# A three-stage attention, gated MLP and expert kernel: three widths of an expert's first-layer group for five, and four buffers for raw weights for two

## The chip, the cores and the metric

The kernel runs on one core of a Trainium2 chip. The metric is the device time of one execution in microseconds (us). The comparison is with the kernel before the change, 794.81 us as the median of three runs.

## What is computed

Four sequences of 576 tokens go through an attention with 8 heads of 64 (with a bias from running sums of `s`), a gated MLP over a width of 512, and a layer of 8 experts, of which each token uses one. The expert layer, the one that the change touches, is cut from the reference here:

```python
logits = np.einsum('bsd,de->bse', x, w_gate)
...
for b in range(B):
    prev_e = -1
    for s in range(S):
        fresh_e = int(np.argmax(logits[b, s]))
        ...
        h = np.maximum(x[b, s] @ w1[e], 0.0)
        out[b, s] = p[e] * (h @ w2[e])
```

`w1[e]` is 512 x 1024 and `w2[e]` 1024 x 512. A second gate decides whether a token takes its own best expert or that of the token before it. How many of the 2304 tokens an expert gets is known only on the chip.

## The kernel before, in words

The program is one stream of instructions for each engine. A scheduler puts them in order when the program is built, from its own estimate of times, within what data, buffers and a few `behind(...)` lines allow; each engine then runs its stream in that order. Attention, the MLP and the routing take the first 500 us and some; the change doesn't touch them. Before the MLP has ended, expert 0's first 256 tokens are fetched and their first layer is run (`early_fetch`, `early_xT`, `early_L1`, lines 1387 to 1409). Its result, the early hT, is a tile `hTA` of 128 x 2 x 8 x 256 numbers in the pool `wpool`; `early_L2` reads it.

**Tokens.** For each expert up to three blocks of 128 tokens are gathered by an indirect DMA on POOL (`gather`, line 1275), turned with PE into `xT` (line 1281), and split there into a rounded high part and the rest, since every product is made of three: high x high, high x rest, rest x high.

**Weights.** `load_w(e, j)` (line 1244) brings one eighth of an expert's weights, 512 KB: `j` 0 to 3 are the first layer's, 4 to 7 the second's. SP issues the DMA into a raw buffer (`wraw`, two of them), ACT casts it into the high part of a `wp` tile (line 1256), and DVE subtracts to get the rest (line 1257). The raw buffer is free when DVE is done, the `wp` tile (ten in turn, four in one pool and six in the other) when PE has used it. `next_w` says in `experts` (line 1438) where each load stands: (e,6), (e,7), (e+1,0) and (e+1,1) after the groups `LW` of expert e's first layer, (e+1,2) and (e+1,3) after it, (e+1,4) and (e+1,5) after its second layer.

**First layer.** `L1` (line 1310) makes eight groups `f` of 128 hidden units, each of 12 matmuls into one PSUM buffer (`ps`, seven in turn). ACT takes the relu into `hT` (line 1340), DVE the rest (line 1341). For experts 1 to 7 the 12 matmuls stand in the program five times, for 256, 288, 320, 352 and 384 columns of tokens, and PE branches to one by the expert's class `wide[e]`, which `emit_wide` counts from the token numbers (`choose`, lines 1327 to 1337). The first matmul of a group always has 384 columns. In this run the widths of experts 1 to 7 are 384, 320, 256, 288, 288, 320 and 352.

**Second layer.** `L2` (line 1347) makes 128 tokens by 24 matmuls, scales them, and scatters them to the output with an indirect DMA on POOL. The third block has three forms by `tail[e]`: none, a narrow one of 16 matmuls on a copy in a tile `xTA`, or the full 24. In this run expert 3 has none, experts 2, 4, 5 and 6 the narrow one, 1 and 7 the full one. The transposes for the next expert stand between the two layers. Beside expert 3, a few small instructions make a list for tokens beyond three blocks (`emit_olist`).

Expert 0 is not in `wide`. SP's queue is in order: an issue that waits for its raw buffer holds those behind it.

Of the kernel before, what the change touches and what calls it, by code (L numbers as in the profile page):

```python
# [8 lines left out]
F32 = mybir.dt.float32  # L9
# [4 lines left out]
ALU = mybir.AluOpType  # L14
# [10 lines left out]
def f32v(ap):  # L25
    return ap.bitcast(F32)
# [7 lines left out]
def kernel(  # L34
# [19 lines left out]
    PE, ACT, DVE, POOL, SP = nc.tensor, nc.scalar, nc.vector, nc.gpsimd, nc.sync  # L54
# [10 lines left out]
    KD = DM // 128  # L65
# [11 lines left out]
    def dma(out, in_):  # L77
        return SP.dma_start(out=raw(out), in_=raw(in_))
# [3 lines left out]
    def behind(x, name):  # L82

        tc.add_manual_dep(
            x.ins, name, mybir.DependencyInfo(mybir.DependencyClass.NoSync, mybir.DependencyReason.DATA), reason="after"
        )
# [12 lines left out]
    def rs():  # L99
        return ps("rt", 1)  # L100
# [15 lines left out]
    def T(pool, shape, dt, tag, bufs=1):  # L116
        _n[0] += 1
        return pool.tile(shape, dt, tag=tag, name=f"{tag}_{_n[0]}", bufs=bufs)
# [1122 lines left out]

    WP = {}

    def load_w(e, j):

        r = T(wpool, [128, 1024], F32, "wraw", bufs=2)
        if j < KD:
            dma(r, w1[e, 128 * j:128 * j + 128, :])
        else:
            f0 = 256 * (j - KD)  # L1250
            x = dma(r.rearrange("p (a d) -> p a d", a=2), w2[e, f0:f0 + 256, :].rearrange("(a p) d -> p a d", p=128))
            if e == 0:
                behind(x, m_loads[LPN])
        near = (e * 2 * KD + j) % (WA + WB) < WA
        w = T(wpool if near else epool[0], [128, 2, 1024], F32R, "wp", bufs=WA if near else WB)
        c = ACT.copy(out=w[:, 0, :], in_=r)  # L1256
        a = DVE.tensor_tensor(out=w[:, 1, :], in0=r, in1=f32v(w[:, 0, :]), op=ALU.subtract)  # L1257
        if (0, KD) <= (e, j) < (1, KD):
            behind(a, dmarks[-1].ins.name)
        if (1, 0) < (e, j) < (1, 2 * KD):  # L1260
            behind(c, amarks[1 if j < KD else 3].ins.name)
        WP[e, j] = w

    CC = CAP * 128
# [24 lines left out]
            DVE.tensor_tensor(out=xt[:, 1, kt, 0:w], in0=pt[:, 0:w], in1=f32v(xt[:, 0, kt, 0:w]), op=ALU.subtract)  # L1289

    LW = (0, 2, 4, 6)
    WIDE = (256, 288, 320, 352, CC)
    wide, tail = {}, {}

    def emit_wide(pool):

        pt = rs()
        PE.matmul(pt[:, 0:E], lhsT=onesb, rhs=carry, start=True, stop=True)
        cls = T(pool, [128, 2, E], F32, "cls")
        cli = T(pool, [128, E], I32, "cli")  # L1300
        DVE.tensor_copy(out=cls[:, 0], in_=pt[:, 0:E])
        DVE.tensor_scalar(out=cls[:, 1], in0=cls[:, 0], scalar1=float(WIDE[0]), scalar2=None, op0=ALU.is_gt)
        for x in WIDE[1:-1]:
            DVE.scalar_tensor_tensor(out=cls[:, 1], in0=cls[:, 0], scalar=float(x), in1=cls[:, 1], op0=ALU.is_gt, op1=ALU.add)
        DVE.tensor_copy(out=cli, in_=cls[:, 1])
        for e in range(1, E):
            wide[e] = PE.value_load(cli[0:1, e:e + 1])
            tail[e] = nc.values_load(cli[0:1, e:e + 1], engines=[mybir.EngineType.PE, mybir.EngineType.Activation, mybir.EngineType.DVE])

    def L1(e, xt, ht, w_, after={}):  # L1310
        for f in range(NF):
            pt = ps()
            fs = slice(128 * f, 128 * f + 128)

            def products(c):
                pairs = []
                for kt in range(KD):
                    w = WP[e, kt]
                    pairs += [(w[:, 0, fs], 0, kt), (w[:, 0, fs], 1, kt), (w[:, 1, fs], 0, kt)]
                for n, (l, z, kt) in enumerate(pairs):  # L1320
                    a = w_ if n == 0 else c
                    m = PE.matmul(pt[:, 0:a], lhsT=l, rhs=xt[:, z, kt, 0:a], start=(n == 0), stop=(n == len(pairs) - 1))  # L1322
                    if n == 0 and f in after:
                        behind(m, after[f].ins.name)

            if e in wide:
                def choose(a, z):
                    if z - a == 1:
                        products(WIDE[a])
                        return  # L1330
                    m = (a + z) // 2
                    with tc.If(wide[e] < m) as x:
                        choose(a, m)
                    with x.Else():
                        choose(m, z)

                choose(0, len(WIDE))
            else:
                products(w_)
            ACT.activation(out=ht[:, 0, f, 0:w_], in_=pt[:, 0:w_], func=ACTF.Relu)  # L1340
            DVE.scalar_tensor_tensor(out=ht[:, 1, f, 0:w_], in0=pt[:, 0:w_], scalar=0.0, in1=f32v(ht[:, 0, f, 0:w_]), op0=ALU.max, op1=ALU.subtract)  # L1341
            yield 12 * w_ * 0.42
# [218 lines left out]
    for b in range(B - 1):  # L1561
        m = M_steps(b) if b else M0_steps()
# [12 lines left out]
    wpool = wctx.enter_context(tc.tile_pool(name="wpool", bufs=1, side="right"))  # L1575
# [21 lines left out]
    x = fetch(early["xg2"], ids[:, CAP - 1:CAP])  # L1597
# [36 lines left out]
```

## Time and profile before

| | us |
|---|---|
| median of 3 runs (794.74 to 808.97) | 794.81 |
| the profiled execution | 794.49 |
| its span, first to last instruction | 792.6 |
| PE busy in the span | 752.5 |
| DVE, ACT, POOL busy | 527.9, 434.0, 344.5 |
| experts 1 to 7, from 551.67 to about 784 | 232.3 |

The profile comes from one execution, so sums are made against 794.49 us. PE is the matmul engine, DVE the vector engine, ACT the scalar engine; POOL and SP issue DMAs. A matmul's end is modelled, and neighbouring matmuls overlap, so a row's us can reach a little into the next row. "Issue" as a releaser means that the profile shows nothing for which the engine waited. The granted clock is 1.00 at 2.4 GHz and 0.50 at 1.2 GHz. A row of the timeline that merges matmuls of several widths shows the width of the first.

### The profile page before, as it was taken

The page shows a single profiled execution, that of the slowest core. Times are in us where ns is not written, and L with a number is a line of the kernel's source. Part 1 is how long each engine was busy: PE and PEld are TensorE (multiplying, and loading weights), DVE is VectorE, ACT ScalarE, POOL GpSimd, SP SyncE. Part 2 cuts the span into 40 slices and gives each one's busy share as a digit, 9 for nine tenths or more (in the row PEclk, how much of TensorE's full clock was granted, in tenths as well). Part 3 has the DMA queues.
Part 4 walks back from the last instruction along what each step waited for, and adds up shares of the span by engine and source line. Part 5 has one row for each costly group of instructions (what it writes and reads, how often), then busy time and mean ns, then how long its engine had stood idle before and what let it go on. Part 6 is the DMA issues. An engine that isn't in the chain of part 4 may idle for free. (4 is left out here: it accounts for less than half of the span.)

```text
span 792.6 us, 14859 instructions
## 1 busy us (share of the span) xinstructions
PE 752.5 (95%) x4763; PEld 643.7 (81%) x4763; DVE 527.9 (67%) x1493; ACT 434.0 (55%) x1039; POOL 344.5 (43%) x616
## 2 busy tenths in 40 slices
PE   9988998999999999999999999999999789998895
PEld 5666786799889899898898879787988678888694
DVE  6888577885776889696986777675535456555440
ACT  6777676875447876266973354145434444453431
POOL 6688545775525687335784020070122222412211
PEclk9999999999999999999999999999999999999998
DMA  7888689666688485688441952164363553753521
GB/s 184 207 235 238 149 230 280 158 184 158 157 247 220 107 240 120 168 254 198 108 155 33 343 168 94 61 195 167 96 206 101 185 176 128 215 160 122 182 65 38
DMA packets 118066, 133.46 MB, mean 168 GB/s; under 512 B 69603, under 2 KB 83043, under 8 KB 117963
## 3 DMA queue, kind: packets, MB, share of 16 engines
q1 hardware_dynamic: 114123, 122.61, 56.1%
q0 software_dynamic: 3840, 9.48, 3.4%
q8 instruction: 64, 1.05, 0.5%
q14 instruction: 39, 0.32, 0.1%
HBM read 90.99 MB, written 22.95 MB: 144 GB/s over the span
## 5 line engine op out<-in xcount | busy, mean ns | idle before, releaser
L1257 DVE TENSOR_TENSOR wp<-wraw,wp 128x1024 fp32r<-128x1024 f32 x64 | 80.3, 1260 | 72.9 <-ACT wp L1256 65.0
L1322 PE MATMUL ps<-xT,wp 128*128 128x320 f32 (+4 forms) x672 | 106.8, 317 | 13.8 <-issue 8.6
L1322 PEld LDWEIGHTS ps<-xT,wp 128*128 128x128 f32 x672 | 102.6, 193 | 17.6 <-issue 11.1
L1256 ACT CAST wp<-wraw 128x1024 fp32r<-128x1024 f32 x64 | 67.0, 1051 | 78.8 <-DMA wraw<-in_moe_w_dram 76.4
L447 ACT ACTIVATE E<-E,negm 128x128 f32<-128x128 f32 (+4 forms) x136 | 79.2, 584 | 33.7 <-DVE negm L440 21.6
L451 POOL TENSOR_SCALAR E<-E,lsum 128x128 f32<-128x128 f32 (+4 forms) x136 | 81.2, 600 | 36.2 <-DVE lsum L449 29.4
L887 PE MATMUL ps<-wp,hT 128*128 128x512 f32 x408 | 95.7, 394 | 1.2 <-DVE hT L1430 0.6
L887 PEld LDWEIGHTS ps<-wp,hT 128*128 128x128 f32 x408 | 76.0, 188 | 17.9 <-DVE hT L1430 1.1
L572 PE MATMUL ps<-et,vv 128*128 128x320 f32 (+9 forms) x462 | 79.5, 310 | 2.3 <-DVE et L539 1.2
L440 DVE CUSTOM_DVE_ANT_0 E<-ps,zmask 128x128 f32<-128x128 f32 (+4 forms) x136 | 63.5, 471 | 23.4 <-PE ps L887 18.0
L572 PEld LDWEIGHTS ps<-et,vv 128*128 128x128 f32 (+1 forms) x462 | 63.1, 173 | 15.4 <-DVE et L539 2.1
L532 PE MATMUL ps<-ident,E 128*128 128x128 f32 (+1 forms) x452 | 67.9, 262 | 4.8 <-POOL E L451 3.2
L1380 POOL DMA_INDIRECT out_dram<-y,ids x24 | 27.9, 1162 | 95.8 <-ACT y L1357 65.8
L448 POOL TENSOR_SCALAR lsum<-lsum 128x1 f32<-128x1 f32 (+1 forms) x128 | 29.6, 231 | 91.8 <-ACT E L447 79.8
L887 PE MATMUL ps<-wsg,vg 128*128 128x288 f32 x448 | 67.5, 300 | 0.6 <-DVE g L896 0.3
L541 ACT CAST et<-ps 128x384 fp32r<-128x384 f32 (+3 forms) x120 | 50.5, 428 | 29.3 <-PE ps L532 27.9
L887 PEld LDWEIGHTS ps<-wsg,vg 128*128 128x128 f32 x448 | 61.0, 188 | 1.4 <-DVE g L896 0.6
L532 PEld LDWEIGHTS ps<-ident,E 128*128 128x128 f32 (+1 forms) x452 | 47.5, 141 | 15.0 <-POOL E L451 4.9
L542 DVE TENSOR_TENSOR et<-ps,et 128x384 fp32r<-128x384 f32 (+3 forms) x120 | 56.8, 482 | 3.9 <-ACT et L541 3.5
L887 PE MATMUL ps<-w,vg 128*128 128x512 f32 (+1 forms) x216 | 56.8, 403 | 0.0
L887 PE MATMUL ps<-xh,w 128*128 128x288 f32 x240 | 54.9, 306 | 0.8 <-DVE wsg L870 0.7
L1341 DVE SCALAR_TENSOR_TENSOR hT<-ps,hT 128x384 fp32r<-128x384 f32 x56 | 30.0, 552 | 34.6 <-ACT hT L1340 34.6
(329 smaller groups left out, 1615.4 us busy)
## 6 DMA issues: line engine op xcount, KB each, us to landing
wraw<-in_moe_w_dram SPq DMA_DIRECT2D x64, 512.0 KB
qk<-qk SPq DMA_DIRECT2D x24, 432.0 KB
w<-wv_d SPq DMA_DIRECT2D x16, 512.0 KB
w<-wo_d SPq DMA_DIRECT2D x16, 512.0 KB
qk<-qk SPq DMA_DIRECT2D x24, 288.0 KB
w<-wu_d SPq DMA_DIRECT2D x11, 512.0 KB
nq<-in_q_dram SPq DMA_DIRECT2D x30, 144.0 KB
nk<-in_k_dram SPq DMA_DIRECT2D x30, 144.0 KB
```

The costliest lines, as they stand in the source:

```text
L440: hred[g] = DVE.tensor_tensor_reduce(out=e[:, a:z], in0=pt[:, 0:z - a], in1=zmask[:, m0:m0 + z - a], scale=-1.0, scalar=BIG if hi == 0 els ...
L447: ACT.activation(out=x, in_=x, func=ACTF.Exp, scale=-1.0, bias=nm, accum_out=l[:, z:z + 1])
L451: POOL.tensor_scalar(out=x, in0=x, scalar1=l[:, z:z + 1], scalar2=1.0, op0=ALU.mult, op1=ALU.mult)
L532: PE.transpose(pt[:, j * M:(j + 1) * M], e[h, 128 * j:128 * (j + 1)], ident[h, h])
L541: ACT.copy(out=dst[0], in_=src)
L542: DVE.tensor_tensor(out=dst[1], in0=src, in1=f32v(dst[0]), op=ALU.subtract)
L572: PE.matmul(x, lhsT=l, rhs=rhs if g >= F4 else f32v(rhs), start=(j == 0 and n_ == 0), stop=(j == js[-1] and n_ == len(ms) - 1),)
L887: ms = [PE.matmul(pt, lhsT=l, rhs=r, start=(first_ and x == 0), stop=(last_ and x == n - 1)) for x, (l, r) in enumerate(pairs)]
L1256: c = ACT.copy(out=w[:, 0, :], in_=r)
L1257: a = DVE.tensor_tensor(out=w[:, 1, :], in0=r, in1=f32v(w[:, 0, :]), op=ALU.subtract)
L1322: m = PE.matmul(pt[:, 0:a], lhsT=l, rhs=xt[:, z, kt, 0:a], start=(n == 0), stop=(n == len(pairs) - 1))
L1341: DVE.scalar_tensor_tensor(out=ht[:, 1, f, 0:w_], in0=pt[:, 0:w_], scalar=0.0, in1=f32v(ht[:, 0, f, 0:w_]), op0=ALU.max, op1=ALU.subtract)
```

## The change

Three widths are left: 288, 320 and 384. The class is counted against 256, 288 and 320, so an expert with up to 256 tokens now uses 288 columns and one with 321 to 352 uses 384. PE tests class < 2, then class < 3. From the weight (1,6) on, the loads whose number 8e + j is 2 or 3 modulo 4 go into a tile with room for two raw weights, with the tag `hTA`, that is in the place of the early hT; the others go on using the two `wraw` buffers.

```diff
--- before.py
+++ after.py
@@ -1241,9 +1241,18 @@
 
     WP = {}
 
+    RW = 4 * KD - 2
+    raws = []
+
     def load_w(e, j):
 
-        r = T(wpool, [128, 1024], F32, "wraw", bufs=2)
+        n = 2 * KD * e + j
+        if n >= RW and n % 4 > 1:
+            if not raws:
+                raws.append(T(wpool, [128, 2, 1024], F32, "hTA"))
+            r = raws[0][:, n % 2, :]
+        else:
+            r = T(wpool, [128, 1024], F32, "wraw", bufs=2)
         if j < KD:
             dma(r, w1[e, 128 * j:128 * j + 128, :])
         else:
@@ -1289,7 +1298,8 @@
             DVE.tensor_tensor(out=xt[:, 1, kt, 0:w], in0=pt[:, 0:w], in1=f32v(xt[:, 0, kt, 0:w]), op=ALU.subtract)
 
     LW = (0, 2, 4, 6)
-    WIDE = (256, 288, 320, 352, CC)
+    STEP = (256, 288, 320)
+    WIDE = ((2, 288), (3, 320), (4, CC))
     wide, tail = {}, {}
 
     def emit_wide(pool):
@@ -1299,8 +1309,8 @@
         cls = T(pool, [128, 2, E], F32, "cls")
         cli = T(pool, [128, E], I32, "cli")
         DVE.tensor_copy(out=cls[:, 0], in_=pt[:, 0:E])
-        DVE.tensor_scalar(out=cls[:, 1], in0=cls[:, 0], scalar1=float(WIDE[0]), scalar2=None, op0=ALU.is_gt)
-        for x in WIDE[1:-1]:
+        DVE.tensor_scalar(out=cls[:, 1], in0=cls[:, 0], scalar1=float(STEP[0]), scalar2=None, op0=ALU.is_gt)
+        for x in STEP[1:]:
             DVE.scalar_tensor_tensor(out=cls[:, 1], in0=cls[:, 0], scalar=float(x), in1=cls[:, 1], op0=ALU.is_gt, op1=ALU.add)
         DVE.tensor_copy(out=cli, in_=cls[:, 1])
         for e in range(1, E):
@@ -1324,17 +1334,17 @@
                         behind(m, after[f].ins.name)
 
             if e in wide:
-                def choose(a, z):
-                    if z - a == 1:
-                        products(WIDE[a])
+                def choose(a):
+                    m, c = WIDE[a]
+                    if a == len(WIDE) - 1:
+                        products(c)
                         return
-                    m = (a + z) // 2
                     with tc.If(wide[e] < m) as x:
-                        choose(a, m)
+                        products(c)
                     with x.Else():
-                        choose(m, z)
-
-                choose(0, len(WIDE))
+                        choose(a + 1)
+
+                choose(0)
             else:
                 products(w_)
             ACT.activation(out=ht[:, 0, f, 0:w_], in_=pt[:, 0:w_], func=ACTF.Relu)
```

On PE, this is the start of group 0 of expert 1 before: the branches, the version for 256 columns, and the first rows of the next. `wp` are the split weights, `xT` the tokens, `ps` the PSUM buffer.

```order
L1332 COMPARE_AND_BRANCH x2
L1322 MATMUL ps<-xT_8214,wp_8196 128x384
L1322 MATMUL ps<-xT_8214,wp_8196 128x256 x2
L1322 MATMUL ps<-xT_8214,wp_8201 128x256 x3
L1322 MATMUL ps<-xT_8214,wp_8206 128x256 x3
L1322 MATMUL ps<-xT_8214,wp_8211 128x256 x3
L1332 UNCONDITIONAL_BRANCH
L1322 MATMUL ps<-xT_8214,wp_8196 128x384
L1322 MATMUL ps<-xT_8214,wp_8196 128x288 x2
```

The same place on PE now:

```order
L1342 COMPARE_AND_BRANCH
L1332 MATMUL ps<-xT_8213,wp_8195 128x384
L1332 MATMUL ps<-xT_8213,wp_8195 128x288 x2
L1332 MATMUL ps<-xT_8213,wp_8200 128x288 x3
L1332 MATMUL ps<-xT_8213,wp_8205 128x288 x3
L1332 MATMUL ps<-xT_8213,wp_8210 128x288 x3
L1342 UNCONDITIONAL_BRANCH
L1342 COMPARE_AND_BRANCH
L1332 MATMUL ps<-xT_8213,wp_8195 128x384
L1332 MATMUL ps<-xT_8213,wp_8195 128x320 x2
```

The version for 256 columns is gone, and so is the one for 352 further down; the first branch leads straight to 288.

On ACT, these are the first layer of expert 6 before and the rows behind it. `wraw_11931` and `wraw_11936` hold the expert's second-layer weights 0 and 1, `wraw_12018` and `wraw_12157` its weights 2 and 3, `wraw_12296` a first-layer weight of expert 7. `hT_11950` are the relus, `xT_12519` the next expert's tokens.

```order
L1373 UNCONDITIONAL_BRANCH
L1332 UNCONDITIONAL_BRANCH x7
L1256 CAST wp_11933<-wraw_11931 128x1024
L1340 ACTIVATE hT_11950<-ps 128x384 x7
L1256 CAST wp_11938<-wraw_11936 128x1024
L1332 UNCONDITIONAL_BRANCH
L1288 CAST xT_12519<-ps 128x384 x2
L1256 CAST wp_12020<-wraw_12018 128x1024
L1288 CAST xT_12519<-ps 128x384
L1340 ACTIVATE hT_11950<-ps 128x384
L1288 CAST xT_12519<-ps 128x384
L1256 CAST wp_12159<-wraw_12157 128x1024
```

The same place on ACT now. The two casts from `hTA_8329` at the head are the expert's second-layer weights 2 and 3, the next two casts the first-layer weights 0 and 1 of expert 7, and the `hTA_8329` further down its weights 2 and 3.

```order
L1383 UNCONDITIONAL_BRANCH
L1342 UNCONDITIONAL_BRANCH x5
L1265 CAST wp_10933<-hTA_8329 128x1024
L1265 CAST wp_11019<-hTA_8329 128x1024
L1265 CAST wp_11106<-wraw_11104 128x1024
L1265 CAST wp_11193<-wraw_11191 128x1024
L1342 UNCONDITIONAL_BRANCH x2
L1350 ACTIVATE hT_10890<-ps 128x384 x7
L1342 UNCONDITIONAL_BRANCH
L1265 CAST wp_11240<-hTA_8329 128x1024
L1297 CAST xT_11247<-ps 128x384
L1265 CAST wp_11244<-hTA_8329 128x1024
```

Casts have moved from behind the relus to ahead of them: the head of the first layer now holds four instead of one, and they belong to weights that are further ahead in the program.

## Rows read from the trace of the kernel before

**Rows 1.** Stretch table, experts' stage: length, PE PEld DVE ACT POOL busy, clock, DMA, GB/s

```profile
551.67:784.00 232.33, 217.62 (x1207) 193.20 (x1205) 111.07 (x151) 98.41 (x151) 52.60 (x44) 0.99 0.47 144
```

**Rows 2.** Stretch table, experts 1 to 7, cut where their first layers start

```profile
551.67:586.37 34.70, 34.70 (x182) 31.62 (x181) 16.51 (x21) 14.94 (x23) 4.67 (x4) 1.00 0.47 144
586.37:616.67 30.30, 30.30 (x173) 27.21 (x172) 14.27 (x18) 13.46 (x21) 8.80 (x7) 1.00 0.49 145
616.67:649.20 32.53, 26.31 (x172) 23.22 (x170) 18.16 (x29) 14.41 (x24) 8.72 (x8) 1.00 0.54 165
649.20:680.85 31.65, 29.76 (x172) 26.18 (x173) 17.42 (x23) 14.87 (x23) 8.30 (x7) 1.00 0.49 151
680.85:711.35 30.50, 29.73 (x173) 26.12 (x172) 16.11 (x23) 15.05 (x23) 8.34 (x8) 1.00 0.61 178
711.35:744.64 33.29, 31.05 (x174) 27.25 (x172) 16.27 (x22) 14.34 (x22) 7.75 (x6) 1.00 0.45 149
744.64:783.50 38.86, 35.77 (x169) 31.60 (x167) 12.33 (x16) 10.95 (x17) 6.02 (x5) 0.91 0.27 94
```

**Rows 3.** PE's waits from 550 us on: us in total, times, longest

```profile
PE ps L1322 <- issue: 8.6, 6, 2.8
...
PE ps L1322 <- DVE wp L1257: 3.6, 3, 1.8
```

**Rows 4.** Timeline of PE: start, us, line, operation, count, [idle before <-releaser]

```profile
536.68 5.76 PE L887 MATMUL ps<-wp,hTA 128*128 128x512 f32 x24
...
568.48 1.47 PE L1287 MATMUL ps<-ident,xg 128*128 128x128 f32 x12
...
621.40 3.13 PE L1322 MATMUL ps<-xT,wp 128*128 128x256 f32 x24 [1.42 <-issue]
...
625.25 2.96 PE L1322 MATMUL ps<-xT,wp 128*128 128x256 f32 x23 [0.71 <-issue]
...
630.96 1.75 PE L1322 MATMUL ps<-xT,wp 128*128 128x384 f32 x12 [2.75 <-issue]
...
649.20 3.54 PE L1322 MATMUL ps<-xT,wp 128*128 128x384 f32 x24 [1.34 <-issue]
...
654.58 10.49 PE L1322 MATMUL ps<-xT,wp 128*128 128x384 f32 x72 [1.85 <-issue]
...
680.85 8.36 PE L1322 MATMUL ps<-xT,wp 128*128 128x384 f32 x60
...
766.47 16.65 PE L887 MATMUL ps<-wp,hT 128*128 128x512 f32 x72
```

**Rows 5.** Timeline of all engines, from expert 6's second layer into expert 7

```profile
742.53 1.05 ACT L1256 CAST wp<-wraw 128x1024 fp32r<-128x1024 f32 x1 [0.99 <-DMA wraw<-in_moe_w_dram]
...
746.53 1.04 ACT L1256 CAST wp<-wraw 128x1024 fp32r<-128x1024 f32 x1 [1.05 <-DMA wraw<-in_moe_w_dram]
...
747.89 0.76 PE L1322 MATMUL ps<-xT,wp 128*128 128x352 f32 x3 [1.80 <-DVE wp L1257]
...
750.04 16.59 PE L1322 MATMUL ps<-xT,wp 128*128 128x384 f32 x84 [0.52 <-PE ps L1322]
```

**Rows 6.** Stretch table, start of expert 7 (columns as in rows 1)

```profile
748.00:752.00 4.00, 3.10 (x11) 2.51 (x12) 0.97 (x1) 0.42 (x1) 1.84 (x1) 0.66 0.69 213
752.00:756.00 4.00, 4.00 (x15) 4.00 (x15) 1.23 (x1) 1.57 (x2) 0.90 (x1) 0.50 0.51 146
```

**Rows 7.** Timelines of SP (640 to 650) and ACT, second layer of expert 3

```profile
641.45 3.66 SPq L78 DMA_DIRECT2D wraw<-in_moe_w_dram  x2
...
645.09 1.05 ACT L1256 CAST wp<-wraw 128x1024 fp32r<-128x1024 f32 x1 [1.02 <-DMA wraw<-in_moe_w_dram]
...
644.73 3.08 SPq L78 DMA_DIRECT2D wraw<-in_moe_w_dram  x2
...
653.19 1.04 ACT L1256 CAST wp<-wraw 128x1024 fp32r<-128x1024 f32 x1 [2.55 <-DMA wraw<-in_moe_w_dram]
```

**Rows 8.** Page, DMA queues: packets, MB, share of 16 engines

```profile
q8 instruction: 64, 1.05, 0.5%
```

## The prediction

> **What bounds the kernel now.** I read the table of stages first: in the experts' stage (551.67 to 784) PE is busy 217.62 of 232.33 us, the other engines at most half of it [rows 1]. So the time there is PE's own work plus the 14.7 us in which PE stands still, and the order below shows that the programs differ nowhere before this stage. Next I cut the stage at the starts of the seven experts' first layers [rows 2]. Experts 1 and 2 have no idle PE at all; 3 has 6.22 us (32.53 less 26.31), 4 has 1.89, 5 has 0.77, 6 has 2.24, 7 has 3.09. In expert 7's stretch the granted clock is also only 0.91. Which kind of stop it is stands in PE's list of waits: 8.6 us in six stops are "issue" (PE waited for nothing that the profile shows), 3.6 us are waits for a weight that DVE had not split yet [rows 3].
>
> The two kinds lie in different places. The timeline of PE puts nearly all "issue" stops into experts 3 and 4, always between two groups of a first layer, and in expert 3 after every second group: the pieces begin at 616.67, 621.40, 625.25 and 630.96, thus 4.73, 3.85 and 5.71 us apart, while the two groups between them take 3.13 us [rows 2, 4]. The weight waits are at the heads of experts 6 and 7. In expert 7, ACT casts two of the four first-layer weights only at 742.53 and 746.53, both just after a DMA wait (0.99 and 1.05 us), PE stops until 747.89, and then the granted clock falls to 0.66 and 0.50, that is to the 1.2 GHz level, until about 756 [rows 5, 6].
>
> **The change: three versions, not five.** PE's program holds 7,628 matmuls before and 6,284 after (seven experts, eight groups, two versions of twelve left out). The instruction queue with 64 packets and 1.05 MB [rows 8] fits PE: 1.05 MB over two instructions for each of the 7,628 (a weight load and a matmul) is 69 bytes each, an estimate. A packet is 16.4 KB; a group of five versions, 120 instructions, is 8.3 KB, so a packet lasts two groups. That is the very distance of the stops in expert 3. With three versions a group is 72 instructions, 5.0 KB, and a packet lasts 3.3 groups. At expert 5's clean pace, 60 matmuls in 8.36 us or 1.67 us a group of 288 [rows 4], that is 5.5 us for a packet: more than the 4.73 and 3.85 us in which packets came, and 0.2 less than the worst, 5.71. So I cost the code stops at about nothing after.
>
> What the two dropped versions cost: expert 3 goes from 256 to 288 columns. Its two groups at 256 took 3.13 us, 1.565 each; 1.67 less 1.565, times eight, is +0.84 us. Expert 7 goes from 352 to 384 columns; it is taken below at expert 1's pace, which is 384 already. Expert 1 (384), 4 and 5 (288), 2 and 6 (320) keep their width. One DVE comparison less and one branch less a group are costed at nothing: DVE idles half of the stage [rows 1].
>
> **The change: four raw buffers.** With two, a load is issued when DVE has split the weight two before it. From issue to cast it took 3.64 us (641.45 to 645.09), and up to 5.7 us when the second of two issues waited behind the first (second issue about 647.4, cast 653.19) [rows 7]. The order shows what follows: before, one cast stands ahead of expert 6's relus, and the rest of the eight crowds into its second layer and beyond. After, four casts stand there (second-layer weights 2 and 3, and the next expert's first two), and four in the second layer. Each pair loads while the other is cast. So expert 7's first-layer weights are all cast in or before expert 6's second layer, and the stop at 747.89 goes, with the fall of the clock behind it.
>
> What the moved casts can cost: relu 0 of a group now waits for four casts on ACT, 4.2 us. PE goes on, because seven PSUM buffers hold the groups 0 to 6; it stops only if the first relu is not done when group 7 starts, 7 x 1.67 = 11.7 us in. Cost nothing, with 7 us to spare. Upper end: all four loads in series at 5.7 us from about 5 us into the second layer (48 of the 72 matmuls that take 16.65 us, and 1.47 of transposes: 12.6 us, without a tail [rows 4]). The last lands at 27.8, that is 15.2 us into the next first layer: a stop of 3.5 us, in one or two experts. The room of the early hT: its last reader is the PE piece from 536.68, 5.76 us long [rows 4], so the loads there cannot start before 542.4, and the load behind them on SP (expert 1's second-layer weight 1) waits too. It is needed when expert 1's second layer starts, after 568.48 [rows 4]: hidden by 26 us less 6 for landing, cast and split. If that cover were gone, it would cost a few us once.
>
> **The sum**, against the profiled execution's 794.49 us (span 792.6 and 1.9 around it):
> - Expert 3: 26.31 busy + 0.84 = 27.15, against 32.53: -5.4.
> - Expert 4: the idle 1.89 goes. Its eight groups took 3.54 and 10.49 = 14.0 us [rows 4], at 1.67 they are 13.4; I take half of these 0.6: -2.2.
> - Expert 5: 0.77, and 0.3 for its last three groups by the same step: -1.1.
> - Expert 6 becomes what expert 2 is, the same width with the same tail: 33.29 to 30.30, -3.0.
> - Expert 7 becomes expert 1 without the transposes for a next expert, 34.70 - 1.47 = 33.23 [rows 2, 4]; now it takes from 744.64 to 783.12 (766.47 + 16.65), 38.48: -5.2. The wider version is in it.
>
> That is -16.9, so 777.6, and on the median of the runs shown (794.81, 0.3 above the profiled one) 777.9: **778.0 us**. What is late next is PE's own work; I look for nothing behind it. Ends: if the rest of the 0.6 us in experts 4 and 5 goes too and the joins tighten, 774; if a stop of 3.5 us comes in two experts, 785.0.
>
> **Rivals.**
> 1. *The code stops shrink only with the code.* Each packet edge may still stop PE, wherever a jump meets it: 3/5 of the 8.6 us stay, 5.2 us, giving 783.2. For it: the stops are at packet edges. Against it: experts 1, 2 and 6 jump over as many versions, cross as many edges, and have no "issue" stop; they only use a packet more slowly. The Trainium skill ("Runtime: NRT & Kernel Launch", Instruction fetch mechanics) says that code is streamed in 16 KiB blocks by purely sequential prefetch, and that a taken branch whose target is outside the fetched pages stalls for a fetch. By that rule rival 1 would be the case, with 783.2. The packets of 16.4 KB agree; experts 1 and 2 with none of the stalls do not.
> 2. *The weights stay late.* The casts are ordered by the scheduler, and ACT waits for whichever DMA stands first. If the two stops of experts 6 and 7 stay (3.0 and 5.2), and expert 7 is 0.84 wider by the step above, the time is 778.0 + 9.0 = 787.0. For it: all loads still use one queue. Against it: DMA share is 0.45 to 0.61 in every stretch [rows 2], and the order puts the casts earlier.
> 3. *Slower: four standing loads starve PE of code.* If a packet of code must queue behind the weights in flight, twice as many would double its time, from 4.8 us (the mean of the three distances) to 9.5, against the 5.5 us that it lasts. The 56 groups are 17 packets; each us beyond 5.5 costs 17 us, so from 6.5 us on the gain is gone, and at 9.5 us the time is 778 + 68 = 846. For it: expert 3's stops come while weights load. Against it: expert 5 has the highest DMA share, 0.61, and 0.77 us idle; expert 3 has 0.54 and 6.22 [rows 2]. The Trainium skill ("DMA: Bandwidth & Descriptors", Queues, rings and completion order) says that each DMA engine goes round robin between its queues, a packet at a time. By that rule a deeper weight queue leaves the code's queue its turn, and this rival falls; no row here shows the turns themselves.
>
> **Chances.** Forecast 0.66 (774 to 782, two thirds of it below 778.9, which is 2% under the median; 2% is about what a measurement of this kernel can tell from no change). Rival 1 0.17, rival 2 0.10, rival 3 0.07. Faster by over 2%: 0.66 x 0.7 = 0.46. Slower by over 2%: 0.07. The rest, 0.47, lies within. The range that leaves out some 2 in 10 runs from 773.5 to 788, which takes in rivals 1 and 2.
>
> **What would show it.** In the changed kernel's list of PE's waits, "issue" before the first layer's products should be under 1 us, and the waits for a split weight gone; the clock 1.00 through expert 7; expert 3 some 27.2 us, 6 some 30.3, 7 some 33.2 to its last matmul. SP should issue loads in pairs, and ACT's waits for raw weights should fall well under half. I am wrong if "issue" stops stay at packet edges (rival 1), if a first layer's head still waits for DVE (rival 2), or if experts 1 and 2, clean now, get stops (rival 3).

## The result, and the profile after

The changed kernel takes 781.31 us as the median of four executions (780.34 to 782.03), beside 794.77 us for the kernel before. The ratio is 0.9844, with a 95% interval from 0.9811 to 0.9878: faster by 1.6%, clear of no change, but within the 2% that the prediction took as the bound. The forecast was 778.0 us, the range 773.5 to 788. The profiled execution took 780.34 us (span 778.5), against the 777.6 of the sum. Ratios leave out an execution that stood out as slow at a low granted clock; medians are of all.

These lines of the page of the changed kernel answer to [rows 8] and to the groups of products and splits:

```profile
PE 749.2 (96%) x4763; PEld 641.2 (82%) x4763; DVE 525.0 (67%) x1492; ACT 432.6 (56%) x1039; POOL 357.7 (46%) x616
...
q8 instruction: 52, 0.85, 0.4%
...
L1332 PE MATMUL ps<-xT,wp 128*128 128x288 f32 (+2 forms) x672 | 102.7, 313 | 1.1 <-PEq L1384 1.1
```

PE's own work is nearly as long as before (749.2 us for 752.5; in the profile before, part of expert 7 ran at the lower clock); what went is mostly the time in which it stood. PE's code is 52 packets, not 64. The 672 products of the experts' first layers, with 8.6 us of "issue" before them in [rows 3], now have 1.1 us of idle time in one piece.

The stretch table of the changed kernel, cut at the starts of the seven first layers as [rows 2] (length, busy PE, PEld, DVE, ACT, POOL, clock, DMA share, GB/s), ends at expert 7's last product:

```profile
552.07:586.79 34.72, 34.72 (x181) 31.62 (x180) 17.46 (x21) 14.96 (x24) 5.76 (x4) 1.00 0.50 159
586.79:617.10 30.31, 30.31 (x173) 27.19 (x172) 16.56 (x21) 14.94 (x23) 9.45 (x7) 1.00 0.55 181
617.10:645.23 28.13, 27.06 (x172) 24.10 (x170) 17.88 (x30) 14.89 (x23) 12.01 (x8) 1.00 0.60 183
645.23:674.33 29.10, 29.10 (x172) 26.06 (x173) 15.78 (x21) 14.36 (x22) 9.89 (x7) 1.00 0.59 188
674.33:704.71 30.38, 29.28 (x173) 25.98 (x172) 16.85 (x23) 14.83 (x23) 11.62 (x7) 1.00 0.54 177
704.71:735.52 30.81, 30.55 (x173) 27.14 (x172) 16.85 (x23) 14.96 (x23) 10.57 (x6) 1.00 0.43 144
735.52:768.84 33.32, 33.32 (x169) 30.00 (x167) 7.80 (x12) 7.81 (x13) 5.56 (x5) 1.00 0.07 27
```

The seven experts take 216.77 us. Cut in the same way, those before took 231.45 (551.67 to 783.12), so the seven take 14.7 us less, in experts 3 to 7, as the prediction placed it. That is the whole gain of the profiled executions (14.15 us; the stage starts 0.4 us later). Of it 11.4 us are idle time of PE and 3.3 us busy time. Experts 1 and 2 are what they were. The clock is 1.00 in expert 7, where it was 0.91.

PE's waits from 550 us on, in all, times and longest, answer to [rows 3]:

```profile
PE ps L1296 <- DMA xg<-x_d,ids: 1.4, 2, 1.1
PE ps L1332 <- PEq L1384: 1.1, 1, 1.1
```

No wait of PE put down to "issue" or to a split weight is left. What is left shows in the timeline of PE (start, us, line, operation, count, [idle before <-releaser]):

```profile
645.23 13.32 PE L1332 MATMUL ps<-xT,wp 128*128 128x384 f32 x96 [1.07 <-PEq L1384]
...
688.81 1.42 PE L1296 MATMUL ps<-ident,xg 128*128 128x128 f32 x11 [1.10 <-DMA xg<-x_d,ids]
...
735.52 16.83 PE L1332 MATMUL ps<-xT,wp 128*128 128x384 f32 x96
752.19 16.65 PE L887 MATMUL ps<-wp,hT 128*128 128x512 f32 x72
```

Each first layer is one row of 96 products now (expert 3's is parted only by the list's small products). The 1.07 us before expert 4 stand at the branch on `tail` (L1384), behind the tail forms that expert 3 doesn't use; in [rows 4] the same place is the 1.34 at 649.20, there called "issue". The trace has PE's sequencer (what hands PE its instructions) step by step there: it waits for the last product of expert 3, jumps over the forms (0.29 us), loads the next expert's class (0.31) and tests it, with no product left to run meanwhile. The two waits for `xg`, the gathered tokens, are new: PE has caught up with POOL's gathers.

### The profile page after: what moved, and what is told of

The parts are those of the page before. It is cut to its first block, busy times and chain, and to the rows that moved or that the text cites. A ratio compares the mean times of both kernels' runs of the same rounds, so it can differ in the third digit from the quotient of the medians.

```text
span 778.5 us, 14818 instructions
## 1 busy us (share of the span) xinstructions
PE 749.2 (96%) x4763; PEld 641.2 (82%) x4763; DVE 525.0 (67%) x1492; ACT 432.6 (56%) x1039; POOL 357.7 (46%) x616
## 5 line engine op out<-in xcount | busy, mean ns | idle before, releaser
L1332 PE MATMUL ps<-xT,wp 128*128 128x288 f32 (+2 forms) x672 | 102.7, 313 | 1.1 <-PEq L1384 1.1
L1390 POOL DMA_INDIRECT out_dram<-y,ids x24 | 30.2, 1257 | 88.0 <-ACT y L1367 52.8
L1266 DVE TENSOR_TENSOR wp<-wraw,wp 128x1024 fp32r<-128x1024 f32 x38 | 47.2, 1261 | 18.2 <-ACT wp L1265 14.7
L887 PE MATMUL ps<-w,xh 128*128 128x512 f32 (+1 forms) x160 | 51.0, 400 | 0.3 <-DVE negm L440 0.3
L887 PE MATMUL ps<-qk 128*128 128x128 f32 (+1 forms) x192 | 50.4, 347 | 0.4 <-DVE negm L440 0.2
```

Of the source, the lines that this page charges most:

```text
L887: ms = [PE.matmul(pt, lhsT=l, rhs=r, start=(first_ and x == 0), stop=(last_ and x == n - 1)) for x, (l, r) in enumerate(pairs)]
L1390: POOL.indirect_dma_start(out=of[:, :], out_offset=bass.IndirectOffsetOnAxis(ap=idx, axis=0), in_=y, in_offset=None, bounds_check=NT - 1, ...
```

## The experiments

| kernel | median, us | kernel before on the same chip | ratio, 95% interval |
|---|---|---|---|
| changed kernel again | 780.74 | 800.36 | 0.9741 [0.9682, 0.9799] |
| three versions, two buffers | 782.85 | 800.36 | 0.9793 [0.9743, 0.9843] |
| five versions, four buffers | 788.66 | 800.36 | 0.9858 [0.9808, 0.9909] |
| three widths, code as long as five | 787.68 | 800.36 | 0.9838 [0.9768, 0.9908] |
| kernel before again | 797.92 | 798.99 | 0.9967 [0.9931, 1.0004] |
| before, early casts | 791.72 | 798.99 | 0.9897 [0.983, 0.9963] |
| three versions, reversed | 782.64 | 798.99 | 0.9783 [0.9717, 0.985] |
| third gather buffer | 784.27 | 798.99 | 0.9794 [0.9723, 0.9865] |
| three versions, late cast | 783.55 | 800.50 | 0.9769 [0.9703, 0.9836] |
| changed, late cast | 780.76 | 800.50 | 0.974 [0.9678, 0.9802] |
| changed, two late splits | 785.91 | 801.86 | 0.9817 [0.9763, 0.987] |

They ran on four other chips. There the kernel before takes 799 to 802 us, the changed one the same 781; the last section comes back to this. Kernels are compared within a chip.

### The two halves apart

The changed kernel once more, for its spread:

> The changed kernel once more, as the base of this set. Both theories: 780 to 782.5 us, no wait of PE for a split weight, under 1.5 us of stops without a releaser in the experts' first layers.

It gave 780.74 us, as expected. Then only the three versions, with the two raw buffers of before:

```diff
-        n = 2 * KD * e + j
-        if n >= RW and n % 4 > 1:
...
-            r = raws[0][:, n % 2, :]
-        else:
-            r = T(wpool, [128, 1024], F32, "wraw", bufs=2)
+        r = T(wpool, [128, 1024], F32, "wraw", bufs=2)
```

> Only the first half of the change: three versions, but the two raw buffers of before. Theory A (the two halves remove different stops): PE's stops without a releaser in the first layers fall from 8.6 us to under 2, its waits for split weights stay or grow (3.6 us before, 3 to 8 here), the clock still falls at an expert's head; 784 to 789 us. Rival B (the raw buffers do nothing, the code was all): 780 to 782.5 us. Rival C (weights are the bound and the code stops only hid behind them): 792 to 795 us.

It took 782.85 us (781.41 to 784.33): 17.5 us less than before, of the 19.6 that both halves give there. PE's waits, then the row of its timeline at expert 7:

```profile
PE ps L1323 <- PEq L1375: 1.1, 1, 1.1
PE ps L1323 <- DVE wp L1257: 0.9, 1, 0.9
PE ps L1323 <- ACT wp L1256: 0.3, 1, 0.3
PE ps L1323 <- PE ps L1323: 0.2, 1, 0.2
```

```profile
736.72 16.83 PE L1323 MATMUL ps<-xT,wp 128*128 128x384 f32 x96
```

The code stops are gone, as expected. But so is the stop at expert 7's head, with two buffers; the 1.4 us of weight waits are all at expert 6's head. The time lies between the 784 to 789 us expected of two separate halves and the rival's 780 to 782.5: the weight waits fell by themselves. So four buffers are not needed to take away the larger stop. Then only the four buffers, with the five versions of before (the removed lines above put into the kernel before):

> Only the second half: five versions, four raw buffers. Theory A: the waits for split weights and the fall of the clock in expert 7 go (about -8 us together with expert 6, and expert 7 keeps its 352 columns), the stops without a releaser stay at 6 to 10 us; 785 to 789 us. Rival B: 793 to 796 us. Rival D (four loads in flight starve PE of code): the stops without a releaser grow to over 12 us and reach experts 1 and 2; over 792 us.

It took 788.66 us (787.57 to 789.24), within the 785 to 789 expected. PE's waits, then two stretches over experts 1 and 2:

```profile
PE ps L1331 <- issue: 6.9, 4, 2.9
PE ps L1331 <- DVE hT L1350: 1.5, 1, 1.5
```

```profile
551.00:585.00 34.00, 34.00 (x178) 31.06 (x178) 17.81 (x23) 15.91 (x24) 4.97 (x4) 1.00 0.50 169
585.00:617.00 32.00, 32.00 (x180) 28.59 (x180) 16.11 (x21) 14.94 (x23) 9.45 (x7) 1.00 0.57 179
```

The weight waits go, the code stops stay in experts 3 and 4 (the 1.5 us before expert 5's last group, put down to DVE, are code too: that DVE operation had ended 6 us before PE went on, and the sequencer was still at the end of the group before; the next section has how code shows). Expert 7's first layer is one row again. PE is busy through all of experts 1 and 2 with four loads standing. The halves alone give 17.5 and 11.7 us, together 19.6: both take the same stops at experts 6 and 7.

### Is it the length of the code, or the jumps?

Three widths, but with two dead copies more of the widest version, so that the program is as long as before:

```diff
-                        products(c)
+                        with tc.If(wide[e] < m) as x:
+                            products(c)
+                        with x.Else():
+                            products(c)
+                            products(c)
```

> The changed kernel with two more copies of the 384 version that no expert uses, behind the third: the code of five versions, the widths of three. An expert of 288 or 320 columns takes as many jumps as in the changed kernel. Theory A (the stops come from how fast PE uses up packets of code): stops without a releaser return, 4 to 10 us, most in the 288 experts 3, 4 and 5, none in 1 and 7; 785 to 791 us. Rival E (the number of jumps made them): within 1 us of the changed kernel.

Its median is 787.68 us. One of its four executions took 797.00; the other three, 784.98 to 788.88, have 786.49 in the middle, 5.75 more than the changed kernel beside it and within the 785 to 791 expected. The profile is of the one of 786.49. PE's code is 63 packets. PE's waits:

```profile
PE ps L1332 <- issue: 2.4, 4, 1.6
PE ps L1332 <- DVE hT L1355: 1.9, 1, 1.9
PE ps L1332 <- PEq L1388: 1.0, 1, 1.0
PE ps L1296 <- issue: 0.5, 1, 0.5
PE ps L1332 <- PE ps L1332: 0.3, 1, 0.3
```

Dead code brings stops back: 2.9 us of "issue", and 1.9 us put down to a DVE operation that had ended over 7 us before PE went on. They came in experts 1, 2, 4, 5 and 6, not in expert 3, where they were expected too; at 288 columns that one ran clean here. An expert of 288 or 320 columns jumps as often as in the changed kernel. So length is the cause, but the place of a stop can't be told from the pace of a group alone.

The traces show the waiting itself. These lines are of PE's branches in `choose`, from the kernel before, the changed one, this one and the next one below (how often, then the shortest, the middle and the longest in ns):

```profile
L1332 PEldq COMPARE_BRANCH  x176: 65/208/4592, 548.8 to 763.8; - x176
L1342 PEldq COMPARE_BRANCH  x128: 65/179/609, 549.3 to 747.3; - x128
L1346 PEldq COMPARE_BRANCH  x128: 65/208/4144, 550.3 to 753.8; - x128
L1342 PEldq COMPARE_BRANCH  x136: 65/174/393, 551.3 to 747.8; - x136
```

A test that doesn't jump takes 65 to 70 ns, a jump mostly 170 to 220. In the kernel before, 12 branches take more than 500 ns, and each of them ends 1.35 to 1.49 us after a packet of the instruction queue, 16,384 bytes, has landed. The longest begins at 626.06 behind a group of expert 3 and ends at 630.65; a packet landed at 629.25. PE worked off products already handed to it until 628.20 and then stood until 630.96. The other code stops of [rows 3] end in the same way, 1.35 to 1.7 us after a packet landed, three of the five inside a version, away from any jump. Only the 1.34 us at 649.20 don't: the last packet had landed 13.8 us earlier. So of the 8.6 us of "issue", 7.2 were waits for code. Experts 2 and 6 of the kernel before have such jumps too, of up to 1.72 and 2.70 us; the products handed over before hid the two of expert 2 entirely.

Then a run that was to have the versions in the order 384, 320, 288, so that the narrow experts jump twice in code as long as in the changed kernel:

```diff
-                    with tc.If(wide[e] < m) as x:
-                        products(c)
+                    with tc.If(wide[e] < WIDE[a - 1][0]) as x:
+                        choose(a - 1)
                     with x.Else():
-                        choose(a + 1)
+                        products(c)
...
```

> The changed kernel with its three versions in the program as 384, 320, 288. The code has the same length; an expert of 288 columns now jumps twice to reach its version, one of 384 runs the first. Theory A (length of code by time): within 1.5 us of the changed kernel, no stops without a releaser beyond 1.5 us. Rival E (jumps): stops of 3 us and more return in experts 3, 4 and 5, over 784 us.

It took 782.64 us (780.99 to 787.45). PE's waits:

```profile
PE ps L1332 <- issue: 1.2, 1, 1.2
PE ps L1296 <- DMA xg<-x_d,ids: 0.2, 1, 0.2
```

The 1.2 us are those at expert 3's unused tail, before expert 4. But the edit doesn't do what it was meant to. The branch of an `If` stands ahead of its `Else` in the program, as the program of the kernel before shows, so the nesting of the edit leaves the versions in the order 288, 320, 384 and only puts both tests ahead of them. In expert 3's groups the trace has two tests of 65 ns that don't jump and one jump, where the changed kernel has one test and one jump: 136 branches in all for 128. So this run shows that one test more in a group costs nothing that can be seen (782.64 us, 1.9 over the changed kernel on another chip; within 1.5 was expected); it says nothing on the number of jumps. What speaks against that number is the run before this one, with stops at the same number of jumps, and the stops that lie away from any jump.

### What the stop at expert 7's head was

The kernel before once more, with a profile on the chip of this set:

> The kernel before once more, with a profile on the chip of this set, since its time stood at 794.8 us in one set and 800.4 in another while the changed kernel kept to 781. Theory A: PE's stops without a releaser and the stop with the fall of the clock are what varies: their sum in the experts' stage is larger than the 14.7 us of the first profile by about what the time is longer. Rival: the stage is the same and the rest of the program is slower. 792 to 802 us.

It took 797.92 us. The profile fell on the slowest of its executions, 812.57 us, and neither of the stops is longer there: "issue" is 8.0 us, weight waits 3.6, and expert 7's stops came again (1.80 and 0.38 us). Its extra time lies outside the stops, as the rival had it; the last section comes back to it. In the kernel before, ACT has the cast of expert 7's weight 3 behind the branches of expert 6's tail, and DVE, whose timeline these rows are from, has the splits of both weights 2 and 3 behind the tail's `y`:

```profile
745.51 0.68 DVE L1366 TENSOR_TENSOR y<-y,ps 64x512 f32<-64x512 f32 x1 [2.65 <-ACT y L1365]
...
746.63 2.35 DVE L1257 TENSOR_TENSOR wp<-wraw,wp 128x1024 fp32r<-128x1024 f32 x2
```

The tail's `y` needs PE's last tail product, which ends where expert 7's first layer begins (744.64). So PE ran into weights that DVE could not have split in time, and weight 2 was cast by 743.58. Weight 3 was late by its data as well: ACT's cast of it at 746.53 waited for the DMA [rows 5]. The changed kernel's DVE has the two splits at 718.97 and 721.47, the `y` at 736.40. The scheduler chose both orders. The next kernel is the one before, with one line of order: a full block's `y` behind the cast of the next expert's weight 3.

```diff
...
+        casts[e, j] = c
...
-            ACT.activation(out=y, in_=pt, func=ACTF.Copy, scale=prob)
+            x = ACT.activation(out=y, in_=pt, func=ACTF.Copy, scale=prob)
+            if narrow is None and (e + 1, KD - 1) in casts:
+                behind(x, casts[e + 1, KD - 1].ins.name)
```

> The kernel before (five versions, two raw buffers) with one edge more for the scheduler: the scaling of each block of a second layer stands behind the cast of the next expert's last first-layer weight. So that cast stands ahead of the second layer's outputs on ACT, in expert 6 too, where it stood behind the narrow block. Theory F (the stop at expert 7 came from the place of that cast, which either half of the change moves): the waits of PE for split weights fall under 1.5 us, the clock stays at 1.00 in expert 7, the code stops stay; 3 to 7 us under the kernel before. Rival (it came from the two buffers): within 1.5 us of the kernel before.

It took 791.72 us (788.89 to 796.52), 7.3 less than the kernel before beside it; 3 to 7 were expected. PE's waits, and its timeline at experts 6 and 7:

```profile
PE ps L1323 <- issue: 6.3, 7, 2.3
PE ps L1323 <- DVE wp L1258: 2.1, 1, 2.1
PE ps L1323 <- PE ps L1323: 1.5, 4, 0.6
```

```profile
712.27 0.43 PE L1323 MATMUL ps<-xT,wp 128*128 128x320 f32 x1 [2.10 <-DVE wp L1258]
...
744.84 15.69 PE L1323 MATMUL ps<-xT,wp 128*128 128x384 f32 x96
```

With five versions and two buffers kept, expert 7 runs clean; the code stops stay, and so does expert 6's wait (2.1 us, where under 1.5 was expected). The line moves more than one split: expert 6's second cast of a second-layer weight now stands ahead of its relus (716.92; before, 727.44), each later cast and load comes a place earlier, and weight 3 of expert 7 is cast at 742.27. So this run takes away the order and the late data together.

Then the reverse: a version without the stop, and the order of before put back. First the cast and the split of weight 3 only, written into each form of expert 6's tail, behind its `y`:

```diff
+        if (e, j) == (7, KD - 1):
+            later.append((r, w))
+            WP[e, j] = w
+            return
         c = ACT.copy(out=w[:, 0, :], in_=r)
...
-            ACT.activation(out=y[0:64], in_=pt[64:128], func=ACTF.Copy, scale=1.0)
+            x = ACT.activation(out=y[0:64], in_=pt[64:128], func=ACTF.Copy, scale=1.0)
+            rest(x)
```

> Three versions and two raw buffers, with one more edit: the cast and the split of the first-layer weight 3 of expert 7 stand behind the y of expert 6's tail, where the kernel before has them on ACT. Theory F (the stop at expert 7's head came from the place of that cast alone): y of the tail ends about when expert 7's first layer starts, cast 1.05 and split 1.3 follow, so PE, which wants this weight some 1.6 us into the first group (nine of 96 products of 16.83 us), stops for about 1 to 2 us, the granted clock falls behind it as it did before, and expert 7 takes 2 to 5 us more: 785 to 788 us, against 782.85 for the same kernel without the edit, and 1 to 2 us of waits for a split weight in PE's list. Rival (the stop came from late data or from code, and three versions took it away by their own): the cast finds its data there and costs under 0.5 us: 782.5 to 783.5.

> The changed kernel, three versions and four raw buffers, with the same edit: the cast and the split of expert 7's first-layer weight 3 stand behind the y of expert 6's tail. Theory F: the weight lies in its raw buffer long before, and still PE stops for 1 to 2 us, with the fall of the clock: 783 to 786 us, against 781. Rival (four buffers take the stop away because the data is there early, as the prediction had it): under 0.5 us: 780.5 to 781.5.

They took 783.55 and 780.76 us: no difference from the kernels without the edit (on another chip) that these runs can tell. That is less than the 785 to 788 and 783 to 786 expected, and within 0.1 us of what the rivals gave (782.5 to 783.5 and 780.5 to 781.5). The profiles show a stop of the same length in both; this is the changed kernel's row:

```profile
739.76 0.44 PE L1336 MATMUL ps<-xT,wp 128*128 128x384 f32 x1 [0.81 <-DVE wp L1366]
```

Expert 7's first layer, from its start to the second layer's, takes 18.58 us in both (737.07 to 755.65, 736.50 to 755.08), against 16.67 in the changed kernel (735.52 to 752.19): +1.9. One late weight does stop PE, but it is not the whole stop. So both splits were put behind the `y`, in the changed kernel:

```diff
+        if (e, j) == (7, KD - 2):
+            later.append((r, w))
+            WP[e, j] = w
+            return
         a = DVE.tensor_tensor(out=w[:, 1, :], in0=r, in1=f32v(w[:, 0, :]), op=ALU.subtract)
...
```

> The changed kernel, three versions and four raw buffers, with DVE in the order of the kernel before at one place: the splits of expert 7's first-layer weights 2 and 3 both stand behind the y of expert 6's tail, and the cast of weight 3 too. One late weight cost 0.81 and 0.2 us of stops and left the clock at 1.00. Theory F2 (the stop before was two splits behind the tail on DVE, whatever the buffers): the head of expert 7 stops for 1.8 + 0.4 + 0.5 us, some 2.7 in all, as in the kernel before, although the data is there early; expert 7's first layer, from its first product to the second layer, takes 19.4 us for 16.8 (and up to 22 if the granted clock falls, as it did in one of two profiles of the kernel before); the time is 783 to 786 us. Rival (the stop needs late loads too, and four buffers take it away): no more than the 1.0 us of one late weight, 780.5 to 782 us.

It took 785.91 us (784.27 to 789.18), within the 783 to 786 expected; the changed kernel did not run on this chip, so the profile decides. DVE and PE in the timeline:

```profile
743.03 0.48 DVE L1397 TENSOR_SCALAR y<-y,xg 64x512 f32<-64x512 f32 x1
743.43 2.35 DVE L1371 TENSOR_TENSOR wp<-hTA,wp 128x1024 fp32r<-128x1024 f32 x2
```

```profile
741.44 1.58 PE L1340 MATMUL ps<-xT,wp 128*128 128x384 f32 x8
744.70 0.80 PE L1340 MATMUL ps<-xT,wp 128*128 128x384 f32 x3 [1.68 <-DVE wp L1371]
745.83 0.44 PE L1340 MATMUL ps<-xT,wp 128*128 128x384 f32 x1 [0.34 <-DVE wp L1371]
746.48 14.83 PE L1340 MATMUL ps<-xT,wp 128*128 128x384 f32 x84 [0.21 <-PE ps L1340]
761.15 16.65 PE L887 MATMUL ps<-wp,hT 128*128 128x512 f32 x72
```

This is the pattern of [rows 5], eight products, a stop, three, a stop, with four buffers and the data long there. Expert 7's first layer takes 19.71 us, 3.0 more than in the changed kernel. So the order on DVE is enough for the stop, whatever the buffers. The clock did not fall here.

### Does the clock always fall behind that stop?

> The kernel before once more, for an undisturbed profile on another chip. If its stops are the same in length everywhere, issue is 8 to 9 us and expert 7's stretch 38 to 39 us, and the execution takes 794 to 796 us. If they are longer where the median was 799 to 800 us, issue is 10 us or more, or the clock in expert 7 is low for longer.

The profiled execution took 794.11 us, as expected. The same place in its stretch table, beside [rows 6]:

```profile
748.00:752.00 4.00, 1.39 (x6) 0.64 (x4) 3.06 (x4) 1.04 (x1) 2.53 (x1) 1.00 0.22 36
752.00:756.00 4.00, 3.83 (x24) 3.84 (x24) 1.22 (x1) 1.05 (x1) 0.00 (x0) 1.00 0.87 295
```

The stops are the same (1.80, 0.39 and 0.59 us), and the clock stays at 1.00. The first layer of expert 7 takes 19.24 us (746.76 to 766.00), not 21.83 (744.64 to 766.47): the fall cost 2.6 us, and it does not always come. With that expert 7 takes 35.9 us here; 38 to 39 were expected.

### The new wait for the gathered tokens

A third buffer for the gathered tokens, in what is left of the early hT's room, in the changed kernel:

```diff
-                xg = xgs[e % 2][:, t] if e else early["xg2"]
+                xg = xgs[e % 3][:, t] if e else early["xg2"]
...
+        room = T(wpool, [128, 2048 + CAP * ROW], F32, "hTA")
```

> The changed kernel with a third buffer for gathered tokens, in what is left of the early hT's room, so that a gather need not wait for the second layer two experts back. In the changed kernel PE waits 1.1 and 0.3 us for gathered tokens in experts 5 and 6. If the buffer was what held the gathers, these go: 778.5 to 780.5 us. If POOL's own order holds them (the gathers stand between scatters that wait for each other), nothing changes: 780 to 782.

It took 784.27 us (780.88 to 787.39), no gain, where 778.5 to 780.5 was expected of the buffer. The waits for `xg` are gone, but a new one is there. PE's waits, and DVE's timeline in expert 3:

```profile
PE ps L1332 <- DVE hT L1351: 1.9, 1, 1.9
```

```profile
627.81 0.18 DVE L1186 CAST olist<-rt 1x31 int32<-1x31 f32 x1 [6.03 <-PE rt L1185]
...
632.45 1.93 DVE L1351 SCALAR_TENSOR_TENSOR hT<-ps,hT 128x384 fp32r<-128x384 f32 x4
```

Here the wait is real. The list's small steps moved ahead of the four splits, DVE stood 6.03 us in them, DVE's part of the first relu came at 632.45, and PE got its PSUM buffer for the eighth group at 633.14. The edit moved the order again.

## Why the prediction was right, and where not

**Place and size.** Sum −16.9 us, measured −14.7 between the experts' starts and ends. By expert (forecast, measured): 3, 27.15 and 28.13; 4, 29.45 and 29.10; 5, 29.4 and 30.38; 6, 30.30 and 30.81; 7, 33.23 and 33.32.

**The change: three versions, not five** was right. The code stops went to nothing, by the cause that was given: dead code alone brings stops back, and the stops end when a packet of code has landed. Rival 1 falls: the longest branch in `choose` is 0.61 us, and PE doesn't stand behind it. What was said against it was not right, though: of the experts that "cross as many edges" with no stop of PE, expert 2 does wait at them, 1.72 and 1.28 us, only PE had products to run meanwhile. The Trainium skill ("Runtime: NRT & Kernel Launch", Instruction fetch mechanics) says that a taken branch out of the fetched pages stalls until its target is fetched. The long jumps of the kernel before, in expert 2 too, agree. Whether it is the length run through or the length jumped over that counts, these runs don't separate: dead code adds to both. The packets' lasting 5.5 us was enough; that the 3.3 us of two groups with five versions are always too short is not borne out, since expert 3 ran clean with the long code (its longest jump there, 1.18 us, was hidden).

**The change: four raw buffers** was wrong in its cause, and right in its time because the scheduler's order changed along with it. "Expert 7's first-layer weights are all cast in or before expert 6's second layer, and the stop goes" is what happened, but two buffers and three versions do it as well, and so do five versions with one line of order. What stood there was two splits behind the tail's `y` on DVE, and that order alone makes the stop again with four buffers; the prediction read ACT's DMA waits in [rows 5] as the cause and did not look at what stood ahead of the splits on DVE. How much the late data of weight 3 would have cost in a better order is not shown. Over the three versions, four buffers take away the 1.4 us of expert 6's head; the medians, 780.74 against 782.85, have intervals that overlap. Rival 2 falls: no weight is late in the changed kernel.

**The fall of the clock** was taken to follow from the stop. It was so in the profile at hand; 2.6 us of what expert 7 lost hang on it, and in another execution it does not come.

**The moved casts** cost nothing in the changed kernel, as said. The third gather buffer shows the price when the cover goes: 1.9 us, in one expert.

**"I look for nothing behind it"** is the step that made the forecast too low. In the profiled execution 2.7 us are missing. 1.07 of them are the sequencer's steps at expert 3's unused tail, which the prediction had among expert 3's 6.22 us of code stops and took off with them; 1.36 are the gathers (1.10 and 0.26), which came late once PE was faster.

**Rival 3**, four loads that starve PE of code, falls: experts 1 and 2 have no idle PE with five versions and four buffers, and the "issue" of that kernel is 6.9 us, not more than 8.6. A packet of code took 1.04 us of transfer there in the middle of those in the experts, 0.96 before: not twice as long. The Trainium skill ("DMA: Bandwidth & Descriptors", Queues, rings and completion order) has each DMA engine take turns between its queues; this agrees with it.

## What to carry to other kernels

In this kernel a version of a loop body that never ran still cost time: set the bytes of all versions against the time that the one that runs takes, above all for the smallest one. A profile's "issue" can be read further: here the branches' own times and the landings of the instruction queue's packets told waits for code from the rest. Before a stop is put down to a missing buffer, look at what stands ahead of the late instruction on every engine of its chain; here one line of order, with two buffers, did what four buffers seemed to do. A change in the code's length also shifts a scheduler's choices, so each half of a change is to be run alone; and the program that an edit makes is to be read before its run is taken as a test.

## What the runs showed of the hardware

The kernel before is slower on the other chips (799 to 802 us for 794.8), and the changed one is not. The cores' mean granted clock goes with it: on those chips the kernel before was at 0.972 to 0.993 in the executions compared, in the middle 0.983; the changed kernel at 0.987 to 0.996 (0.990 to 0.994 on the first chip). On the chip of the third profile of before, 794.11 us came with 0.993, the other seven executions had 0.975 to 0.987 and 797.75 to 805.84 us. So some of the larger ratio there is clock. Where in an execution it is lost, a profile can show; the changed kernel with two late splits lost it in the attention, which no edit touches. Its first 200 us, and those of the changed kernel in its first profile:

```profile
0.00:100.00 100.00, 93.52 (x582) 63.91 (x583) 71.71 (x240) 65.98 (x184) 69.63 (x144) 0.95 0.79 196
100.00:200.00 100.00, 94.31 (x664) 85.29 (x663) 74.90 (x228) 70.91 (x194) 60.47 (x117) 0.95 0.74 197
```

```profile
0.00:100.00 100.00, 92.27 (x600) 63.93 (x601) 72.38 (x245) 68.03 (x191) 71.28 (x146) 0.98 0.82 201
100.00:200.00 100.00, 94.63 (x688) 84.21 (x685) 76.62 (x239) 71.92 (x199) 64.17 (x124) 1.00 0.76 203
```

By expert 1 the former is 6.2 us behind (558.23 for 552.07). So of the 8.8 us between these two profiled executions 6.2 were lost before the experts and 3.0 in expert 7; the spread of some 4 us between the executions of most kernels here may be of this kind too. One profile of the kernel before on another chip, that of 812.57 us, shows it as well: the clock is 0.88 in its first 100 us, expert 1 starts at 565.46 for 551.67, and so 13.8 of its 18.1 us over the first profile lie before the experts. That was the slowest of its 11 executions; whether the same makes the usual 799 to 802 us there stays open.
